# Subtracting the low halves of converted weights on VectorE instead of GpSimd, from the end of attention on

## The chip, the cores and the metric

The kernel runs on one core of a Trainium2 chip. The metric is the device time of one execution, in microseconds (us); lower is better. A core has four engines that compute, each with an instruction queue of its own that it works through in order: TensorE (matmul and transpose), VectorE, ScalarE and GpSimd. SyncE issues the transfers. In the profile they are called PE (PEld for its weight loads), DVE, ACT, POOL and SP.

## The reference

Attention with rotary embedding over 4 batches of 8 heads, 576 positions of 64 channels; its output, 2304 tokens of 512 channels, goes through two feed-forward blocks. The inputs come as float64 for the weights of the blocks, and the result is float32.

```python
scores = np.matmul(q_rot, k_rot.transpose(0, 1, 3, 2)) / np.sqrt(D)
attn = softmax(scores)                       # over the last axis
x = (attn @ v).transpose(0, 2, 1, 3).reshape(2304, 512)
h = x @ w_in                                 # 512 -> 2048
x2 = (h - np.tanh(h)) @ w_out                # 2048 -> 512
a, b = x2 @ w1, x2 @ w2                      # 512 -> 1024, twice
out = ((a * b) @ w3) @ w_o2                  # 1024 -> 1024 -> 512
```

## The kernel before, in words

TensorE works on a reduced float32 type. To keep accuracy each operand is kept as two halves: the high half is the value rounded to that type, the low half is what is left, value minus high half. A product of two operands is three matmuls: high by high, high by low, low by high.

*Weights.* They arrive as raw float64 words in units of 128 x 512. `load_raw` issues a unit's transfer into one of two `raw` buffers. `to_f32` makes float32 of it with two ScalarE instructions (L117, L119) and two VectorE instructions (L120, L122), in one of three `z` buffers. `split` makes the halves: the high one is a ScalarE copy (L127), the low one a subtraction (L128) on GpSimd. `next_conv` calls `to_f32` for the next unit of a fixed order and issues the next load; `place` and `conv_o2` call `split`. There are 16 units each in the first, second and third half of the weights (w_in and w_out twice, then w1 and w2), and 8 units of w_out2. The 16 units of w3 are not split here: they are transposed on TensorE and multiplied with w_out2 (`wp_trans`, `wp_mm`, L615 to L642), so that the second block needs one product less; L642 is a subtraction on GpSimd of its own.

*Attention.* 80 steps, one for each block of queries. A step has the scores (L325), their maximum on VectorE (L329), the exponential on ScalarE (L336), the scaling by the reciprocal of the sum on GpSimd (L347), transposes (L383, L393) and, for every second or third step, the product with v (L407, L410). Every sixth step converts and places one unit of the first half, nine units in all.

*The first block.* 80 chunks: two halves of the 2048 hidden channels, in each half five blocks of tokens (four of 512 and one of 256), in each block eight chunks of 128 hidden channels. `emit_h` is the product with w_in (L546, 12 matmuls), `emit_g` makes h - tanh(h) with four ScalarE instructions (L559 to L562), four VectorE instructions (L563 to L566), and splits the result with a ScalarE copy (L568) and a VectorE subtraction (L569). `emit_x2` is the product with w_out (L583, 12 matmuls). h and g are made two chunks ahead of x2. Behind each chunk stands what `at` put there: the seven units that are left of the first half in chunks 0 to 3, w_out2 in chunks 3 to 6 of the half, the folding of w3 after it, and the units of the next half from chunk 25 of the half on, at most two per chunk near its end. The tokens x are split too, by `split_x`, both instructions on GpSimd (L528, L529), into six buffers of which one block takes four.

*The second block.* 40 chunks: a and b (L750), their product on VectorE (L756), its split (L758 on ScalarE, L759 on VectorE), the last product (L773).

The order on each engine isn't wholly the order of the program text: the framework plans every queue at build time with costs of its own, and moves an instruction ahead when its inputs are there, of the units left from the first half, for example, some into attention. It also picks the engine of a copy that is written with `nc.any`.

Of the kernel before, what the change touches and what calls it, by code (L numbers as in the profile page):

```python
# [13 lines left out]
ALU = mybir.AluOpType  # L14
# [29 lines left out]
def fused_kernel(tc, q, k, v, w_in, w_out, w1, w2, w3, w_o2, tables, out):  # L44
    nc = tc.nc
# [13 lines left out]
    def f32(ap):  # L59
        return ap.bitcast(F32)  # L60
# [45 lines left out]
    def to_f32(u, z=None):  # L106
# [16 lines left out]
            z, hi, -0x80000000, z, ALU.bitwise_and, ALU.bitwise_or)  # L123
        return z.bitcast(F32)

    def split(z, s):
        nc.scalar.copy(s[:, 0, :], z)  # L127
        nc.gpsimd.tensor_tensor(s[:, 1, :], z, f32(s[:, 0, :]), ALU.subtract)  # L128


    pairs = [(b, hp) for b in range(B) for hp in range(NP)]
# [311 lines left out]
    def place(u):  # L443
        s = slot(slot_of[u], u)
        split(zs.pop(u), s)
        wslot[u] = s
# [63 lines left out]
            pv(b, hp, c // 2)  # L510
    att.release()
    psum.release()


    ph2 = tc.alloc_tile_pool(name="ph2", bufs=2, side="right", reuse_waits="tile")
# [83 lines left out]
    def conv_o2(i, r):  # L599

        u = next_conv()
        if r % 2 == 0:

            if i == 0:
                t = ph2.tile([128, 2, 2, 512], F32R, tag=f"x2{3 - r // 2}", name=f"o2_{i}{r}", bufs=1)
            else:
                t = xpool.tile([128, 2, 2, 512], F32R, tag=f"x{r // 2}", name=f"o2_{i}{r}")
            o2[i, r], o2[i, r + 1] = t[:, 0], t[:, 1]
        split(zs.pop(u), o2[i, r])
# [250 lines left out]
```

## Time and profile before

| | us |
|---|---|
| median of 3 runs | 1117.77 (1115.21 to 1119.29) |
| the profiled execution | 1111.25 |
| its span, from the first to the last instruction | 1109.4 |

| engine | busy in the span | instructions |
|---|---|---|
| TensorE | 95% | 5598 |
| TensorE weight loads | 77% | 5598 |
| VectorE | 66% | 1300 |
| ScalarE | 54% | 1262 |
| GpSimd | 35% | 379 |

Attention takes the first 323 us, the first block goes to about 809 us, the second to the end. A busy share says how much of a stretch an engine had an instruction running; an instruction that is held up while it runs counts as busy. In a view of instructions, idle time stands in brackets with what ended it.

### The profile page before, as it was taken

How to read it: one execution, taken by the hardware profiler on the slowest of the kernel's cores; microseconds unless marked ns; L12 is line 12 of the kernel's file. 1: busy time of each engine (PE TensorE's matmuls, PEld its weight loads, DVE VectorE, ACT ScalarE, POOL GpSimd, SP SyncE). 2: the span in 40 equal slices, each digit the busy share in tenths (PEclk: the TensorE clock that was granted, in tenths of full speed). 3: DMA queues.
4: the chain of work that ended last, by engine and by line, in shares of the span. 5: the costliest groups of instructions: out<-in, count | busy, mean ns of one | idle time of the engine just before them, and what ended most of it. 6: DMA issues, size and time to landing. Idle time of an engine off the chain costs nothing.

```text
span 1109.4 us, 15634 instructions
## 1 busy us (share of the span) xinstructions
PE 1055.3 (95%) x5598; PEld 853.6 (77%) x5598; DVE 730.3 (66%) x1300; ACT 598.9 (54%) x1262; POOL 387.8 (35%) x379
## 2 busy tenths in 40 slices
PE   5999999999998999998989999999799999999998
PEld 3777776777766888887767788898588888888887
DVE  6899988999649867669998867678952212212121
ACT  4688777777767655557767655556652111111121
POOL 5576675665461302014463220323630202001000
PEclk9899999999998999999999999999999999999999
DMA  6667675766403011023223102232740100101010
GB/s 195 171 161 173 182 178 140 186 176 147 99 20 106 10 57 58 32 64 95 77 76 113 38 10 76 87 105 86 246 133 1 38 1 1 38 1 38 1 38 20
DMA packets 64684, 96.36 MB, mean 87 GB/s; under 512 B 11616, under 2 KB 40288, under 8 KB 64608
## 3 DMA queue, kind: packets, MB, share of 16 engines
q1 hardware_dynamic: 64608, 95.38, 30.0%
q8 instruction: 44, 0.72, 0.3%
q14 instruction: 32, 0.26, 0.1%
HBM read 58.79 MB, written 11.01 MB: 63 GB/s over the span
## 4 chain that ended last, share of the span: by engine, by line
PE 68%; DVE 14%; ACT 7%; POOL 4%; DMA 4%; issue 2%; SPq 0%; DVEq 0%; ACTq 0%; POOLq 0%
PE pw L750 18%; PE x2p L583 11%; PE h L546 10%; PE o L773 9%; PE sc L325 6%; PE pv L410 4%; PE wp L630 3%; PE te L383 3%; DVE nm L329 2%; DMA raw_w<-in_moe_w 2%; DVE g_q L564 2%; ACT e L336 1%; DVE g_q L566 1%; PE pv L407 1%; DVE g_s L563 1%
## 5 line engine op out<-in xcount | busy, mean ns | idle before, releaser
L583 PE MATMUL x2p<-g,s_out 128*128 128x512 f32 (+1 forms) x960 | 223.4, 380 | 22.3 <-ACT g L568 12.8
L583 PEld LDWEIGHTS x2p<-g,s_out 128*128 128x128 f32 x960 | 172.2, 194 | 62.8 <-ACT g L568 18.3
L347 POOL TENSOR_SCALAR e<-e,r 128x576 f32<-128x576 f32 x144 | 121.8, 859 | 80.9 <-DVE r L345 35.8
L756 DVE TENSOR_TENSOR ab<-a,pw 128x512 f32<-128x512 f32 (+1 forms) x40 | 25.4, 635 | 182.9 <-PE pw L750 180.5
L336 ACT ACTIVATE e<-sc,nm 128x576 f32<-128x576 f32 x144 | 108.0, 750 | 47.2 <-DVE nm L329 31.5
L329 DVE TENSOR_REDUCE nm<-sc 128x1 f32<-128x576 f32 x144 | 106.8, 749 | 17.3 <-PE sc L325 16.5
L773 PE MATMUL o<-wpt,abs 128*128 128x512 f32 x432 | 104.5, 389 | 0.0
L325 PE MATMUL sc<-ks,qs 128*128 128x288 f32 x480 | 92.1, 321 | 3.2 <-ACT e L336 2.8
L563 DVE TENSOR_TENSOR g_s<-g_s,h 128x512 f32<-128x512 f32 (+1 forms) x80 | 50.5, 632 | 65.8 <-ACT g_m L562 65.6
L773 PEld LDWEIGHTS o<-wpt,abs 128*128 128x128 f32 x432 | 80.6, 188 | 16.4
L325 PEld LDWEIGHTS sc<-ks,qs 128*128 128x128 f32 x480 | 68.8, 190 | 26.7 <-ACT e L336 10.6
L383 PE MATMUL te<-ident,e 128*128 128x128 f32 x576 | 84.4, 278 | 5.1 <-POOL e L347 4.5
L754 ACT COPY a<-pw 128x512 f32<-128x512 f32 (+1 forms) x40 | 21.8, 544 | 117.9 <-PE pw L750 117.9
L568 ACT CAST g<-g_q 128x512 fp32r<-128x512 f32 (+1 forms) x80 | 46.1, 576 | 59.0 <-DVE g_q L566 58.6
L383 PEld LDWEIGHTS te<-ident,e 128*128 128x128 f32 x576 | 68.0, 142 | 11.7 <-POOL e L347 8.4
L559 ACT ACTIVATE g_s<-h 128x512 f32<-128x512 f32 (+1 forms) x80 | 44.1, 551 | 53.9 <-PE h L546 52.4
L569 DVE TENSOR_TENSOR g<-g_q,g 128x512 fp32r<-128x512 f32 (+1 forms) x80 | 58.1, 726 | 22.6 <-ACT g L568 21.7
L566 DVE COPY_PREDICATED g_q<-g_m,g_t 128x512 f32<-128x512 int32 (+1 forms) x80 | 69.1, 864 | 1.6
L758 ACT CAST abs<-ab 128x512 fp32r<-128x512 f32 (+1 forms) x40 | 23.0, 576 | 84.8 <-DVE ab L756 84.8
L564 DVE SCALAR_TENSOR_TENSOR g_q<-g_q,g_s 128x512 f32<-128x512 f32 (+1 forms) x80 | 62.6, 782 | 0.0
L560 ACT ACTIVATE g_q<-g_s,qb 128x512 f32<-128x512 f32 (+1 forms) x80 | 54.5, 682 | 0.2 <-DVE g L569 0.2
L562 ACT ACTIVATE g_m<-g_s,nt 128x512 f32<-128x512 f32 (+1 forms) x80 | 54.0, 676 | 0.0
(380 smaller groups left out, 2256.7 us busy)
## 6 DMA issues: line engine op xcount, KB each, us to landing
ks<-kp SPq DMA_DIRECT2D x60, 288.0 KB, 5.0
raw_w<-in_moe_w SPq DMA_DIRECT2D x32, 512.0 KB, 3.7
raw_in<-in_moe_w_in SPq DMA_DIRECT2D x16, 512.0 KB, 4.0
raw_out<-in_moe_w_out SPq DMA_DIRECT2D x16, 512.0 KB, 4.4
qs<-qp SPq DMA_DIRECT2D x60, 128.0 KB, 3.5
wp_dram<-wpe SPq DMA_DIRECT2D x24, 256.0 KB, 2.0
k<-in_k SPq DMA_DIRECT2D x16, 256.0 KB, 3.2
q<-in_q SPq DMA_DIRECT2D x16, 256.0 KB, 3.0
```

The lines of the kernel that those rows point to most:

```text
L325: nc.tensor.matmul(s[:, n, 0:HS], lhs, rhs, start=t == 0, stop=t == len(terms) - 1)
L329: nc.vector.tensor_reduce(nm[:, j:j + 1], s[:, :, 0:HS], AX.XY, ALU.max, negate=True)
L336: nc.scalar.activation(d["e"][:, j, :].rearrange("p (n s) -> p n s", n=2), d["ss"][j][:, :, 0:HS], AF.Exp, bias=d["nm"][:, j:j + 1], accum ...
L347: nc.gpsimd.tensor_scalar(d["e"][:, j, :], d["e"][:, j, :], r[:, j:j + 1], 1.0, ALU.mult, ALU.mult)
L383: nc.tensor.transpose(ps[:, n * 128:(n + 1) * 128], e[:, o + n * 128:o + (n + 1) * 128], ident)
L546: nc.tensor.matmul(ps[:, 0:w], ws[:, a, kk], x[:, b_, 0:w], start=kc == 0 and t == 0, stop=kc == NK - 1 and t == 2)
L563: nc.vector.tensor_tensor(s, s, h, ALU.mult)
L564: nc.vector.scalar_tensor_tensor(qq, qq, QC, s, ALU.add, ALU.mult)
L566: nc.vector.copy_predicated(qq, mk.bitcast(I32), t)
L583: nc.tensor.matmul(x2ps[j][o][:, 0:w], ws[:, a, oo], g[:, b_, 0:w], start=c == 0 and t == 0, stop=c == HF - 1 and t == 2)
L750: nc.tensor.matmul(ps[:, 0:w], ws[:, a, kk], x[:, b_, 0:w], start=kc == 0 and t == 0, stop=kc == NK - 1 and t == 2)
L773: nc.tensor.matmul(outps[j][t], g[:, a, tt], wp[c][:, b_, :], start=c == 0 and i == 0, stop=c == NF2 - 1 and i == 2)
```

## The change

A list of one element holds the engine that subtracts the low half. It is GpSimd until all of attention has been written, and VectorE from there on. All calls of `split` after the attention loop therefore emit their subtraction for VectorE. `split_x` (L528, L529) and L642 stay on GpSimd, L127 stays on ScalarE.

```diff
+    lows = [nc.gpsimd]
+
     def split(z, s):
         nc.scalar.copy(s[:, 0, :], z)
-        nc.gpsimd.tensor_tensor(s[:, 1, :], z, f32(s[:, 0, :]), ALU.subtract)
+        lows[0].tensor_tensor(s[:, 1, :], z, f32(s[:, 0, :]), ALU.subtract)
...
     att.release()
     psum.release()
+    lows[0] = nc.vector
```

## Rows read from the trace of the kernel before

**Rows 1.** The page, its first part: busy time of each engine.
```profile
PE 1055.3 (95%) x5598; PEld 853.6 (77%) x5598; DVE 730.3 (66%) x1300; ACT 598.9 (54%) x1262; POOL 387.8 (35%) x379
```

**Rows 2.** Stretches: length, busy (instructions) PE PEld DVE ACT POOL, clock, DMA.
```profile
0.00:323.00 323.00, 298.51 (x2028) 224.61 (x2030) 277.03 (x637) 233.32 (x590) 197.99 (x216) 0.98 0.61 157
323.00:345.00 22.00, 17.82 (x70) 13.88 (x67) 17.83 (x18) 13.95 (x25) 13.11 (x11) 0.84 0.14 48
345.00:505.00 160.00, 159.91 (x788) 134.88 (x787) 114.10 (x182) 95.77 (x179) 26.67 (x25) 1.00 0.17 54
515.00:585.00 70.00, 62.76 (x263) 48.44 (x262) 64.38 (x84) 51.84 (x93) 34.10 (x25) 0.98 0.26 79
585.00:630.00 45.00, 42.04 (x179) 32.79 (x178) 38.38 (x55) 31.71 (x57) 15.38 (x13) 1.00 0.25 81
752.00:806.00 54.00, 47.08 (x208) 38.44 (x207) 48.40 (x63) 36.93 (x66) 24.41 (x19) 0.95 0.50 171
806.00:845.00 39.00, 39.00 (x170) 32.16 (x170) 20.65 (x29) 18.16 (x32) 11.37 (x9) 0.98 0.29 94
```

**Rows 3.** The same view of the GpSimd instructions of L128 alone.
```profile
0.00:323.00 323.00, 19.05 (x14) 0.98 0.61 157
515.00:585.00 70.00, 23.05 (x16) 0.98 0.26 79
752.00:806.00 54.00, 11.51 (x8) 0.95 0.50 171
```

**Rows 4.** Line L128: durations min/median/max in ns; who waited for it.
```profile
L128 POOL TENSOR_TENSOR s_in<-z_in,s_in x14: 1272/1302/1751, 24.7 to 573.7; 128x512 fp32r<-128x512 f32 x14
  ACT z_in L117: 8.5, 3
```

**Rows 5.** Timeline from 323 to 345: start, length, instruction, [idle before, releaser].
```profile
323.58 0.62 ACT L127 CAST s_out<-z_out 128x512 fp32r<-128x512 f32 x1 [2.53 <-issue]
326.64 1.31 POOL L128 TENSOR_TENSOR s_in<-z_in,s_in 128x512 fp32r<-128x512 f32 x1
327.42 4.75 DVE L120 SCALAR_TENSOR_TENSOR z_o<-z_o,raw_o 128x512 int32<-128x512 int32 x1 [3.42 <-ACT z_o L117]
329.22 0.72 ACT L562 ACTIVATE g_m<-g_s,nt 128x512 f32<-128x512 f32 x1
331.00 0.64 POOL L528 TENSOR_SCALAR xs_(0, 1)_1_4659<-x 128x512 fp32r<-128x512 f32 x1
333.80 0.67 DVE L563 TENSOR_TENSOR g_s<-g_s,h 128x512 f32<-128x512 f32 x1
337.89 2.07 PE L583 MATMUL x2p<-g,s_out 128*128 128x512 f32 x4 [4.18 <-ACT g L568]
```

**Rows 6.** Timeline of one chunk, 540 to 548, VectorE and GpSimd.
```profile
541.38 1.19 DVE L564 SCALAR_TENSOR_TENSOR g_q<-g_q,g_s 128x512 f32<-128x512 f32 x1
541.99 1.74 POOL L128 TENSOR_TENSOR s_in<-z_in,s_in 128x512 fp32r<-128x512 f32 x1
542.77 1.51 DVE L120 SCALAR_TENSOR_TENSOR z_out<-z_out,raw_out 128x512 int32<-128x512 int32 x1 [0.19 <-ACT z_out L117]
545.44 0.68 DVE L120 SCALAR_TENSOR_TENSOR z_in<-z_in,raw_in 128x512 int32<-128x512 int32 x1
546.04 0.68 DVE L569 TENSOR_TENSOR g<-g_q,g 128x512 fp32r<-128x512 f32 x1
```

**Rows 7.** Timeline from 553 to 569, GpSimd, TensorE and ScalarE.
```profile
554.88 1.30 POOL L128 TENSOR_TENSOR s_out<-z_out,s_out 128x512 fp32r<-128x512 f32 x1 [2.52 <-ACT s_out L127]
561.66 1.04 PE L546 MATMUL h<-xs_(1, 0)_3_6402,s_in 128*128 128x512 f32 x2 [2.20 <-POOL xs_(1, 0)_3_6402 L529]
567.87 0.67 ACT L117 ACTIVATE z_in<-raw_in 128x512 f32<-128x512 f32 x1 [4.86 <-POOL s_out L128]
```

**Rows 8.** Stretches as in rows 2, at lowered clock.
```profile
336.70:343.40 6.70, 5.51 (x13) 4.34 (x14) 6.60 (x10) 5.27 (x10) 1.60 (x1) 0.50 0.22 83
562.00:565.20 3.20, 3.20 (x9) 2.46 (x8) 3.20 (x6) 1.01 (x2) 3.12 (x3) 0.50 0.46 147
```

## The prediction

> **What bounds the kernel now.** I first read the busy shares [rows 1]: TensorE is busy for 95% of the span, VectorE for 66%, GpSimd for 35%. An average of this kind hides stages, so next come the stretches [rows 2]. From 345 to 505 us TensorE is busy for 159.91 of 160.00 us: there it is the bound, and work taken from or given to VectorE changes nothing, but a delay or a gain made before 345 is carried through. The change can matter only where TensorE waits: 323 to 345 (busy 17.82 of 22.00), 515 to 585 (62.76 of 70.00), 585 to 630 (42.04 of 45.00) and 752 to 806 (47.08 of 54.00). In 515 to 585 and 752 to 806 VectorE has little room left: 64.38 of 70.00 and 48.40 of 54.00. So the change adds work to VectorE exactly where VectorE is fullest, and the question is how much of that fullness is work, and how much is VectorE held up by GpSimd.
>
> The timeline of one chunk answers this [rows 6]. L569, a VectorE subtraction of the same shape and types as the one that moves, took 0.68 us undisturbed, and L120 also took 0.68. Beside a GpSimd L128, L120 took 1.51 and L564 took 1.19; these read two tensors from SBUF. The GpSimd side pays as well: 1.74 us against a median of about 1.30 [rows 4]. The worst case is at 327.42, where one L120 took 4.75 us while five GpSimd instructions went by, two of them L128 and three of them splits of x (the first and the last stand in [rows 5]).
>
> **The change part by part.** *Count.* Of the 56 low halves, 9 are placed inside the attention loop and stay on GpSimd. The other 47 move: 7 left over from the first half, 8 of w_out2, 16 and 16 of the second and third half. Before 323 us there are 14 instances of L128 [rows 3], so 5 of the moved ones were put into attention by the planner; 42 lie after it.
>
> *Removed from GpSimd:* 47 x 1.30 = 61 us of an engine with much idle time, worth nothing in itself. *Added to VectorE:* 47 x about 0.60 us. The instruction lasts 0.68, but in a full queue the next starts 0.60 later (545.44 to 546.04 [rows 6]). That is 28 us: 3 in attention, 3.6 around 323 to 350, 9.6 in 515 to 585 (16 instances [rows 3]), 2.4 in 585 to 630, 4.8 in 752 to 806 (8 instances), 4.8 after.
>
> *Removed from VectorE:* the stretching by L128. In the chunk of rows 6 two units are placed, and the two stretched instructions lost 1.51 - 0.68 = 0.83 and 1.19 - 0.68 = 0.51, together 1.34 us, 0.67 per unit. I take 0.6 per moved unit in the full stretches; the bounds are 0 (a unit placed in idle time) and 1.3 (a whole GpSimd instruction). So 0.60 comes and about 0.6 goes. VectorE's time in 515 to 585 and 752 to 806 stays about equal; collisions of the new subtractions with the GpSimd splits of x, which stay, add some 1 to 2 us in all. The load alone is worth between -2 and +4 us; I take +1.
>
> *Stalls that go.* (a) At 323 to 345. The copies before three moved subtractions begin at 323.58, when VectorE has nothing queued that is long; there they can be done some 2 us before GpSimd did them. L120 at 327.42 then meets the splits of x alone. L563 need not wait till 333.80: its last input, L562, is there at 329.22 + 0.72 = 329.94. That is 3.86 us earlier, against 4.18 us of TensorE waiting at 337.89 [rows 5]. I take 3.5, bounds 0 (the splits of x alone keep VectorE out as long) and 4.2. In 336.70 to 343.40 the granted clock was 0.50, that is 1.2 instead of 2.4 GHz [rows 8]; it fell after this wait of TensorE, and it cost half of 6.7 us, 3.4. With a wait under 1 us it may not fall: I take 2, bounds 0 and 3.4. (b) At 561.66 TensorE waited 2.20 us for a split of x on GpSimd. That split came late because L128 stood ahead of it in GpSimd's queue: GpSimd idled 2.52 us for its ScalarE copy and then spent 1.30 on it [rows 7]. With L128 gone the split is done 3.8 us earlier, so the 2.20 goes, and perhaps the 1.6 us which half a clock from 562.00 to 565.20 cost [rows 8]. ScalarE's wait of 4.86 us for a z buffer held by a backed-up L128 [rows 7], of 8.5 us in three such waits [rows 4], goes too, but VectorE is then the next one late: I count 3 for all of (b), bounds 0 and 5. (c) 585 to 630 and 752 to 806: the stalls there come with splits of x and with VectorE's own queue; I count 0, bounds -2 and +3. (d) Attention: 5 x 0.60 more on VectorE, busy 277.03 of 323.00, against 5 x 1.30 less on GpSimd: 0, bounds -1.5 and +2. (e) 806 to 845: VectorE is busy 20.65 of 39.00 and TensorE all 39.00 [rows 2]; 0, bounds 0 and +3.
>
> *One rule against a row.* At 327.42 VectorE was kept out through several GpSimd instructions in a row, 4.75 - 0.68 = 4.07 us [rows 5]. The Trainium skill (SBUF — State Buffer, "SBUF: two separate sides") calls the pair of ports that both engines share an exclusive lock, held for the whole instruction by whichever starts first, which alone would end a wait after the one instruction that is running. By that rule a moved subtraction loses at most one GpSimd instruction, and the load term would end at +2 instead of +4. The row is the longer one and I keep its value for the upper end: a moved subtraction that meets a chain of splits can be held for up to 4 us.
>
> **Sum.** +1 (load) - 3.5 - 2 (a) - 3 (b) + 0 (c, d, e) = -7.5; I take -7, since two terms lean on the next engine being on time. The profiled execution took 1111.25 us, so it would take 1104. The runs shown have a median of 1117.77, 6.5 above that execution; the difference is put onto the median: 1117.77 - 7 = 1111.
>
> **The rivals.** *R1: VectorE takes back what the stalls give.* Waits vanish, but VectorE, with 5.62 us idle in 515 to 585, is the bound there all the same, and the gain at 323 shrinks to 2 or 3 us because the splits of x hold VectorE as before. For it: of the five instructions that L120 waited for at 327.42, three are splits of x [rows 5]. Against it: the balance of 0.60 against 0.67 per unit. Time: -3 to +4, about 1117.
>
> *R2, slower: a new wait at the head of VectorE's queue.* The moved subtraction needs the ScalarE copy L127, which needs L122 on VectorE. GpSimd could sit waiting for L127 at no cost; VectorE cannot, since its queue is in order and L563 to L569 of the next chunk stand behind it. Place: chunks with two units, 515 to 585 and 752 to 806. If nothing useful is queued between L122 and the subtraction, each costs 0.60 plus the copy's 0.62 [rows 5], about 1.2: 24 x 1.2 = 29, minus 24 x 0.6 removed, is 14 more; the idle time of VectorE there (5.6 + 5.6 [rows 2]) covers part of it, as long as it isn't the same idle time that TensorE waits for. With (a) still gained: +7 us, 1125. It decides from about 0.4 us of waiting per moved unit. For it: ScalarE too has a queue, with weight loads ahead. Against it: the planner fills such places, and in the chunk of rows 6 other VectorE work stands there.
>
> *R3: all stalls go, the clock stays up, and VectorE has time left:* -12 to -16, about 1104.
>
> That the change does not do what it says has no room here: the switch is set before the first of the 47 is placed; only where the planner puts them is open.
>
> **How the numbers follow.** Chances: forecast (-4 to -11, around 1111) 0.50; R1 0.25; R2 0.18; R3 0.07. About 0.5%, 5.6 us, is what a measurement of this kernel can tell from no change. Of the forecast's half, 0.38 lies beyond 5.6 us and 0.12 within. Faster: 0.38 + 0.07 = 0.45. Same: 0.12 + 0.25 = 0.37. Slower: 0.18. The range goes from 1102 (R3's far end) to 1125 (the middle of R2); half of R2 (0.09) and some 0.03 below 1102 stay outside, so it should hold a little more than 8 in 10; the terms with bounds on both sides (a, b, the load) make it no narrower.
>
> **What would show it.** Right: no L128 on GpSimd after attention except the nine; L120, L122, L564 and L566 near 0.7 us except beside splits of x; the wait of TensorE near 334 us under 1 us and no half clock after it; no wait of TensorE for a split of x near 560. R1: those stalls shrink, but TensorE's busy share in 515 to 585 stays near 62.76 of 70.00. R2: VectorE idle just ahead of the moved subtractions, ended by L127, over 0.4 us each, and ScalarE waiting for L566 longer than before. The prediction would be wrong by its own steps if the planner orders attention or the chunks otherwise because VectorE now carries the cost, so that places in the timeline no longer answer to each other.

## The result and the profile after

| | before | after |
|---|---|---|
| median, us | 1117.08 (1115.21 to 1119.29) | 1103.62 (1098.54 to 1106.90) |
| the profiled execution, us | 1111.25 | 1106.90 |
| its span, us | 1109.4 | 1105.0 |

The ratio after to before is 0.9875, with an interval from 0.9832 to 0.9918; measured a second time beside the experiments it is 0.9911 (0.9877 to 0.9944). The change makes the kernel about 1% faster, 13.5 us by the medians above. The two profiled executions differ by 4.4 us only; why they show so little of it is said below.

In the changed kernel all line numbers from L127 on are larger: the copy is L129, the low half L130, the split of x L531 and L532, the product with w_in L549, `emit_g` L562 to L572, the product with w_out L586.

The page after, its first part (answers to [rows 1]):
```profile
PE 1060.1 (96%) x5598; PEld 857.8 (78%) x5598; DVE 734.1 (66%) x1344; ACT 599.8 (54%) x1265; POOL 324.2 (29%) x332
```
GpSimd lost 63.6 us and 47 instructions, as counted. VectorE has 44 more (47 subtractions, less three copies that went to ScalarE, 1262 to 1265) and is busy only 3.8 us longer.

The stretches after, with the columns and the times of [rows 2] (length, busy with count of PE, PEld, DVE, ACT, POOL, granted clock, DMA share, GB/s):
```profile
323.00:345.00 22.00, 17.14 (x83) 12.95 (x82) 15.68 (x20) 13.88 (x27) 11.59 (x11) 0.96 0.15 48
345.00:505.00 160.00, 159.89 (x769) 133.76 (x769) 112.73 (x178) 93.37 (x174) 25.12 (x24) 0.99 0.15 50
515.00:585.00 70.00, 67.90 (x304) 55.57 (x303) 66.18 (x102) 53.55 (x97) 14.39 (x12) 0.98 0.22 68
585.00:630.00 45.00, 41.87 (x171) 33.67 (x171) 43.16 (x64) 31.18 (x56) 9.65 (x8) 0.92 0.26 82
752.00:806.00 54.00, 48.59 (x206) 38.46 (x205) 50.71 (x75) 35.30 (x62) 11.01 (x9) 0.94 0.51 174
```
TensorE is busy 67.90 of 70.00 us in 515 to 585, and was 62.76. Its busy time in the other stretches differs by less than 2 us from that before. The work inside a stretch is not quite the same, since the whole run is shifted; so I also take the two parts of the kernel by their own ends.

The first block, from the first matmul of the product with w_in to the end of the last with w_out, before:
```profile
323.44:809.07 485.63, 461.12 (x2179) 381.04 (x2178) 380.76 (x557) 304.31 (x563) 154.04 (x128) 0.98 0.23 77
```
and after:
```profile
327.19:804.58 477.39, 459.24 (x2179) 382.02 (x2178) 381.53 (x590) 303.35 (x562) 105.00 (x94) 0.98 0.24 79
```
It is 8.24 us shorter. TensorE's idle time in it (length less busy) fell from 24.51 to 18.15 us. VectorE ran 33 instructions more in 0.77 us more of busy time: what it lost in held-up time paid for them.

Attention, from the 61st score matmul to the last product with v, before:
```profile
45.68:323.51 277.83, 265.33 (x1878) 201.72 (x1876) 243.77 (x560) 210.12 (x535) 175.34 (x184) 0.99 0.60 152
```
and after:
```profile
54.03:327.26 273.23, 263.64 (x1878) 200.83 (x1876) 242.57 (x563) 210.97 (x537) 171.94 (x179) 1.00 0.62 155
```
That is 4.60 us shorter. The second block is the same to 0.02 us. So this pair differs by 8.24 + 4.60 = 12.8 us, which fits the ratio; 1.3 us of the 4.60 are not the change's, as (d) below shows. The start of the profiled execution after, ahead of these 61 matmuls, took 8.35 us longer than before (54.03 against 45.68), with the same instructions in the same order; that hides most of the gain in the spans. It is the subject of the last section.

TensorE's waits after, by what ended them, 323 to 806 (us in total, times, longest; one of 0.5 us that belongs to attention is left out):
```profile
PE x2p L586 <- ACT g L571: 9.1, 4, 4.4
PE x2p L586 <- DVE g L572: 8.4, 7, 2.4
PE x2p L586 <- DVE x L596: 0.3, 1, 0.3
```
The wait for a split of x of 2.20 us [rows 7] is gone. The longest one is still there, and it is the one that the prediction meant to remove.

Timeline after, 326 to 343 (start, length, instruction, idle before and its releaser), answers to [rows 5]:
```profile
327.99 1.72 DVE L130 TENSOR_TENSOR s_out<-z_out,s_out 128x512 fp32r<-128x512 f32 x1 [0.23 <-ACT s_out L129]
331.17 1.72 POOL L532 TENSOR_TENSOR xs_(0, 1)_0_4596<-x,xs_(0, 1)_0_4596 128x512 fp32r<-128x512 f32 x1
331.66 3.47 DVE L120 SCALAR_TENSOR_TENSOR z_o<-z_o,raw_o 128x512 int32<-128x512 int32 x2
335.77 0.62 ACT L129 CAST o<-z_o 128x512 fp32r<-128x512 f32 x1 [4.33 <-DVE z_o L122]
338.63 0.69 DVE L566 TENSOR_TENSOR g_s<-g_s,h 128x512 f32<-128x512 f32 x1 [1.51 <-ACT g_m L565]
342.30 0.98 PE L586 MATMUL x2p<-g,s_out 128*128 128x512 f32 x3 [4.38 <-ACT g L571]
```
The moved subtractions now collide with the splits of x (1.72 us instead of 0.68), two L120 behind them take 3.47 us beside L532, ScalarE stands 4.33 us on a weight copy that needs their result, and the four ScalarE instructions of the first chunk stand behind that copy. TensorE waits 4.38 us, before 4.18.

Line L130 after 323 us, what the engine waited for ahead of it (us, times):
```profile
  ACT s_w L129: 0.7, 1
  ACT s_out L129: 0.2, 1
```
42 subtractions and 0.9 us of waiting for their copies: 0.02 us each.

### The profile page after: what moved, and what is told of

Same layout as the page of the kernel before. It is cut to its first block, busy times and chain, and to the rows that moved or that the text cites. A ratio compares the mean times of both kernels' runs of the same rounds, so it can differ in the third digit from the quotient of the medians.

```text
span 1105.0 us, 15609 instructions
## 1 busy us (share of the span) xinstructions
PE 1060.1 (96%) x5598; PEld 857.8 (78%) x5598; DVE 734.1 (66%) x1344; ACT 599.8 (54%) x1265; POOL 324.2 (29%) x332
## 4 chain that ended last, share of the span: by engine, by line
PE 69%; DVE 15%; ACT 7%; DMA 4%; issue 3%; POOL 1%; DVEq 0%; ACTq 0%; SPq 0%; POOLq 0%
PE pw L753 18%; PE x2p L586 11%; PE h L549 10%; PE o L776 9%; PE sc L327 7%; PE pv L412 4%; PE wp L633 3%; PE te L385 3%; DVE nm L331 2%; ACT e L338 2%; DMA raw_in<-in_moe_w_in 2%; DVE g_q L569 1%; DVE g_q L567 1%; DVE g L572 1%; PE pv L409 1%
## 5 line engine op out<-in xcount | busy, mean ns | idle before, releaser
L586 PE MATMUL x2p<-g,s_out 128*128 128x512 f32 (+1 forms) x960 | 221.5, 379 | 18.1 <-ACT g L571 9.1
L586 PEld LDWEIGHTS x2p<-g,s_out 128*128 128x128 f32 x960 | 171.9, 193 | 55.9 <-DVE g L572 13.6
L349 POOL TENSOR_SCALAR e<-e,r 128x576 f32<-128x576 f32 x144 | 125.1, 881 | 86.6 <-DVE r L347 46.4
L566 DVE TENSOR_TENSOR g_s<-g_s,h 128x512 f32<-128x512 f32 (+1 forms) x80 | 50.5, 631 | 61.6 <-ACT g_m L565 61.5
L562 ACT ACTIVATE g_s<-h 128x512 f32<-128x512 f32 (+1 forms) x80 | 44.1, 551 | 53.8 <-PE h L549 53.7
L572 DVE TENSOR_TENSOR g<-g_q,g 128x512 fp32r<-128x512 f32 (+1 forms) x80 | 57.4, 717 | 23.3 <-ACT g L571 22.8
L569 DVE COPY_PREDICATED g_q<-g_m,g_t 128x512 f32<-128x512 int32 (+1 forms) x80 | 61.1, 764 | 1.0
L567 DVE SCALAR_TENSOR_TENSOR g_q<-g_q,g_s 128x512 f32<-128x512 f32 (+1 forms) x80 | 55.0, 687 | 0.0
L563 ACT ACTIVATE g_q<-g_s,qb 128x512 f32<-128x512 f32 (+1 forms) x80 | 54.6, 682 | 0.4 <-DVE g L572 0.4
```

The costliest lines, as they stand in the source:

```text
L349: nc.gpsimd.tensor_scalar(d["e"][:, j, :], d["e"][:, j, :], r[:, j:j + 1], 1.0, ALU.mult, ALU.mult)
L567: nc.vector.scalar_tensor_tensor(qq, qq, QC, s, ALU.add, ALU.mult)
L569: nc.vector.copy_predicated(qq, mk.bitcast(I32), t)
L572: nc.vector.tensor_tensor(g[:, 1, 0:w], qq, f32(g[:, 0, 0:w]), ALU.subtract)
L586: nc.tensor.matmul(x2ps[j][o][:, 0:w], ws[:, a, oo], g[:, b_, 0:w], start=c == 0 and t == 0, stop=c == HF - 1 and t == 2)
```

## The experiments

Two theories stood at first. Theory A: the gain is made unit by unit, where a low half on GpSimd held a VectorE operation or stood ahead of a split of x. Theory B: it comes from another plan of the queues. Below, a VectorE operation is called stretched by what it lasted beyond the lower quartile of its line and shape; the sum is over the first block, and what is under 0.05 us is left out. A stretch is put down to the GpSimd instructions that ran beside it, by the length of the overlap. The table holds what was read from the runs: ratio to the kernel before, and from each trace the length of attention and of the first block (with the same ends as above), TensorE's idle time in the block, the time there at a granted clock of 0.50, and the stretch.

| kernel | ratio (95%) | attention | first block | TensorE idle | clock 0.50 | VectorE stretch |
|---|---|---|---|---|---|---|
| before | 1 | 277.83 | 485.63 | 24.51 | 17.1 | 50.9 |
| the change | 0.9875 (0.9832, 0.9918) | 273.23 | 477.39 | 18.15 | 20.5 | 33.6 |
| the change again | 0.9911 (0.9877, 0.9944) | 273.12 | 477.67 | 19.50 | 17.1 | 32.2 |
| first third only | 0.9994 (0.9966, 1.0023) | 273.06 | 486.67 | 25.51 | 17.1 | 46.2 |
| middle third only | 0.9938 (0.9912, 0.9965) | 276.40 | 476.25 | 18.29 | 17.1 | 38.6 |
| last third only | 1.0006 (0.9976, 1.0035) | 277.18 | 483.07 | 20.61 | 17.1 | 44.4 |
| no low halves | 0.9788 (0.9741, 0.9834) | 273.24 | 467.04 | 12.59 | 6.8 | 28.7 |
| w_out2 due later | 0.9907 (0.9877, 0.9937) | 273.13 | 476.54 | 18.18 | 17.1 | 34.2 |
| low half of x alone | 0.9941 (0.9911, 0.9970) | 276.37 | 476.97 | 17.47 | 10.2 | 33.0 |
| change and low half of x | 0.9684 (0.9643, 0.9726) | 273.13 | 452.89 | 3.97 | 0 | 9.2 |
| change and all of x | 0.9718 (0.9680, 0.9756) | 273.21 | 454.84 | 4.93 | 0 | 1.9 |
| change, low x, all low halves | 0.9721 (0.9677, 0.9764) | 273.84 | 453.80 | 4.65 | 0 | 8.6 |
| change and two-input scratch | 1.0149 (1.0109, 1.0189) | 271.80 | 504.69 | 33.56 | 34.1 | 60.6 |
| change and one-input scratch | 0.9996 (0.9966, 1.0025) | 272.52 | 489.01 | 23.76 | 23.9 | 43.3 |

### Which of the moved units bring the gain

Three kernels move one part each; the first:
```diff
-    def split(z, s):
+    def split(z, s, u):
         nc.scalar.copy(s[:, 0, :], z)
-        lows[0].tensor_tensor(s[:, 1, :], z, f32(s[:, 0, :]), ALU.subtract)
+        low = lows[0] if u in half1 + fold[0] else nc.gpsimd
+        low.tensor_tensor(s[:, 1, :], z, f32(s[:, 0, :]), ALU.subtract)
```


> Only the 7 units left over from the first half and the first 4 of w_out2 subtract their low halves on VectorE (11 of the 47); the other 36 stay on GpSimd. Theory A (the gain lies in 515 to 600 us, where VectorE is no longer held up by L128 and the splits of x no longer queue behind it on GpSimd): this part shows only the re-planned attention, -1 to -5 us, 1112 to 1116; the TensorE wait of about 4.3 us behind the first chunk stays. Theory B (the gain is the re-planned attention): nearly the whole gain, 1102 to 1106.

This one moves the seven units that are left of the first half and four of w_out2. The second has `u in half2 + fold[1]` (16 units of the second half, converted from about 508 us on, and four of w_out2), the third `u in half3` (16 units).

> Only the 16 units of the second half and the last 4 of w_out2 subtract on VectorE (20 of 47). Theory A: -6 to -10 us, 1107 to 1111, with TensorE busy over 66 of 70 us in 515 to 585. Theory B: 1116 to 1118, since attention keeps its GpSimd subtractions.

> Only the 16 units of the third half subtract on VectorE. Theory A: 0 to -3 us, 1114 to 1117, since the waits of TensorE near 793 us come with the splits of x, which stay. Theory B: 1116 to 1118. Rival R2 of the prediction (a new wait in VectorE's queue) would show here first: slower by 2 to 4 us.

The middle third measures 0.9938 and the others cannot be told from no change. Its trace has the whole gain of the first block (476.25 against 485.63), with TensorE in 515 to 585 as in the changed kernel:
```profile
515.00:585.00 70.00, 67.20 (x304) 55.39 (x305) 66.43 (x105) 54.72 (x99) 10.87 (x9) 1.00 0.24 76
```
The first third has, by its trace, all of the gain in attention (273.06) and nothing in the block; its ratio alone can't tell this from no change. So there are two separate gains, at two places: theory A holds for the larger, in the block, and attention has one of its own. The last third shows no loss of 2 to 4 us, as R2 would have it. By the measured ratios the parts add up to 0.9938; the whole measured 0.9875 once and 0.9911 once, so whether it is more than its parts stays open.

### How much the low halves cost at all

```diff
-    lows[0] = nc.vector
+    lows[0] = lambda *a: None
...
-                nc.tensor.matmul(ps[:, 0:w], ws[:, a, kk], x[:, b_, 0:w],
+                nc.tensor.matmul(ps[:, 0:w], ws[:, 0, kk], x[:, b_, 0:w],
```
(The other products with split weights are changed alike: the matmul count stays, the low halves of the 47 units are neither made nor read.)

> The 47 low halves are not computed at all, and every product that would read the low half of a weight reads the high half in its place, so that TensorE does as many matmuls of the same shape; this leaves a part of the computation out. It is the bound of what a free subtraction would give. If VectorE pays for the 47 subtractions (my sum: 28 us of its time, of which little shows), this is 3 to 8 us under the changed kernel, 1096 to 1100; if they cost nothing there, it is equal to it, about 1104; if the gain had been used up by them (R1), it is far below, 1090 or less.

It measures 0.9788. So the 47 subtractions cost the kernel before 2.1% where they were, some 23.6 us, and about half of that still where they are now (0.9788 against 0.9875 and 0.9911: 0.9 to 1.2%, 10 to 14 us, 0.2 to 0.3 us a unit). That is more than the 3 to 8 us that were expected; the first blocks of the two traces, 467.04 and 477.39 us, differ by 10.35.

### The changed kernel again

> The changed kernel once more, beside the next three on the same chip, so that its ratio has as many rounds as those of the parts. The low halves of the first third alone gave 0.9994, of the middle third 0.9938, of the last third 1.0006. Theory A (the gain is made where a low half on GpSimd holds a VectorE operation and the splits of x, unit by unit): the parts add up, ratio 0.993 (0.990 to 0.996). Rival B (the parts help one another, since GpSimd comes free for the splits of x only when all are gone, and the plan of attention is another one): ratio 0.9875 as first measured, 6 us better than the sum of the parts.

0.9911, inside theory A's range (0.990 to 0.996); rival B's 0.9875 lies just below the interval, which begins at 0.9877. By itself this does not rule B out. Its trace tells more than its ratio: attention and first block come out as in the first trace to 0.3 us, and its start took 45.50 us up to the 61st score matmul, as in the kernel before, so that its span is 1096.6 us.

### The wait behind the first chunk

```diff
-FOLD_AT, FOLD_EVERY = (3, 10), 2.25
+FOLD_AT, FOLD_EVERY = (5, 10), 2.25
```


> The changed kernel with the conversions of w_out2 due from the fifth place on and not the third. It asks why TensorE's wait of 4.4 us behind the first chunk (337.91 to 342.30) stayed. Theory D (it stays because the planner sets two units of w_out2 ahead of the first chunk's eviction on VectorE, with the splits of x against the moved subtractions): the wait falls under 2 us, 2 to 4 us faster than the changed kernel, ratio 0.984 to 0.986. Rival: the wait is the splits of x behind the moved subtractions, and stays over 3.5 us; ratio as the changed kernel's, within 0.3%.

The wait stays at 4.39 us and the ratio at 0.9907, the figures of the rival. But this decides nothing: the later due place did not move the two L120, which stand in the same order ahead of the first chunk's L566 and last 3.47 us again. The next kernel settles it.

### The splits of x

```diff
         nc.gpsimd.tensor_scalar(t[:, 0, 0:w], src[:, kc, :], 1.0, 1.0, ALU.mult, ALU.mult)
-        nc.gpsimd.tensor_tensor(t[:, 1, 0:w], src[:, kc, :], f32(t[:, 0, 0:w]), ALU.subtract)
+        nc.vector.tensor_tensor(t[:, 1, 0:w], src[:, kc, :], f32(t[:, 0, 0:w]), ALU.subtract)
```


> The changed kernel with the low half of x too on VectorE; the high half stays on GpSimd. Of the 14.5 us that TensorE still waits behind attention in the changed kernel, all stand beside splits of x on GpSimd. Theory A (what is left of the loss is VectorE kept out by these splits, some 33 us of stretched VectorE operations, as it was by the low halves of the weights): 3 to 8 us faster than the changed kernel, ratio to the kernel before 0.981 to 0.985. Rival C (VectorE is full: its busy time in the stretch 515 to 585 is 66 of 70 us by now, so 40 more subtractions of about 0.6 us cost more than the port gives back): 0 to 8 us slower than the changed kernel, ratio 0.988 to 0.995.

0.9684: three times the gain of the change, and far past the expectation of theory A, which counted on a part of TensorE's waits alone and left the half clock out. Rival C falls. The first block of this kernel:
```profile
323.00:775.89 452.89, 448.92 (x2179) 376.51 (x2178) 376.30 (x628) 305.02 (x564) 42.47 (x48) 1.00 0.25 82
```
VectorE has 71 instructions more than in the kernel before (628 against 557) and is busy 4.46 us less. TensorE's idle time falls from 18.15 to 3.97 us, and its busy time by 10.32 us with the same 2179 matmuls; no part of the block is at half clock any more (20.5 us were, which cost half of that, 10.2). In the timeline of its first chunk nothing is held up:
```profile
325.89 0.68 DVE L130 TENSOR_TENSOR s_out<-z_out,s_out 128x512 fp32r<-128x512 f32 x1
329.51 0.69 DVE L566 TENSOR_TENSOR g_s<-g_s,h 128x512 f32<-128x512 f32 x1
333.74 1.43 PE L586 MATMUL x2p<-g,s_out 128*128 128x512 f32 x5
```
L566 begins 6.5 us after the block's start, with the change alone 11.4, and TensorE does not wait. So the wait behind the first chunk was that of VectorE beside the splits of x.

With the high half on ScalarE as well, GpSimd has nothing of x left:
```diff
-        nc.gpsimd.tensor_scalar(t[:, 0, 0:w], src[:, kc, :], 1.0, 1.0, ALU.mult, ALU.mult)
+        nc.scalar.copy(t[:, 0, 0:w], src[:, kc, :])
```


> The changed kernel with the whole split of x off GpSimd: the high half is a ScalarE copy, the low half a VectorE subtraction. Theory A: no VectorE operation is stretched behind attention any more, the waits of TensorE at the heads of the chunks go, 5 to 12 us faster than the changed kernel, ratio 0.977 to 0.983. Rival C: the high halves queue behind the weight copies on ScalarE (some 40 copies of 0.6 us, 23 us) and the low halves behind the products' evictions on VectorE; the chunks begin later, 0 to 10 us slower than the changed kernel, ratio 0.988 to 0.996.

0.9718, faster than theory A's range (0.977 to 0.983); rival C falls. But it is not better than the step before it. The stretch goes from 9.2 to 1.9 us and TensorE's idle time does not fall (4.93), so taking the one-input halves off GpSimd brings nothing more that can be seen, at 18.6 us more on ScalarE (323.61 against 305.02 in the first block). How one VectorE line fares is seen in its row of the page (busy, mean ns, idle before); the copy with a mask, before:
```profile
L566 DVE COPY_PREDICATED g_q<-g_m,g_t 128x512 f32<-128x512 int32 (+1 forms) x80 | 69.1, 864 | 1.6
```
with the change:
```profile
L569 DVE COPY_PREDICATED g_q<-g_m,g_t 128x512 f32<-128x512 int32 (+1 forms) x80 | 61.1, 764 | 1.0
```
and with the change and the low half of x:
```profile
L569 DVE COPY_PREDICATED g_q<-g_m,g_t 128x512 f32<-128x512 int32 (+1 forms) x80 | 56.3, 704 | 0.8
```

Next the same line in the kernel before, the weights' low halves left on GpSimd:
```diff
-        nc.gpsimd.tensor_tensor(t[:, 1, 0:w], src[:, kc, :], f32(t[:, 0, 0:w]), ALU.subtract)
+        nc.vector.tensor_tensor(t[:, 1, 0:w], src[:, kc, :], f32(t[:, 0, 0:w]), ALU.subtract)
```


> The kernel before with one line changed: the low half of x on VectorE, the low halves of the weights left on GpSimd. The change alone measured 0.9875 and 0.9911, both moves together 0.9684. In the trace of the kernel before, VectorE operations behind attention are stretched by 50.9 us, of which 19.5 stand beside low halves of weights and 30.3 beside splits of x. Theory A (each two-input subtraction on GpSimd costs by the VectorE time that it stretches, and the two kinds add): 2.0 to 2.5% without the change, ratio 0.975 to 0.980, and the change on top of it brings about 1%. Rival E (the loss is made where both kinds meet on GpSimd's queue, so taking away either one is nearly enough): ratio 0.968 to 0.972, as with both. Rival F (the low halves of weights on GpSimd then hold more VectorE work than before, since VectorE is fuller): ratio over 0.982.

0.9941. Theory A in its simple form, that the two costs add, is wrong: the change alone brings 0.9 to 1.25%, the low half of x alone 0.6%, both 3.2%. Rival E is wrong too, and F's bound holds, though not for its reason: the stretch by low halves of weights stays at 19.3 us (19.5 before). In the first block the two single moves bring 8.2 and 8.7 us, both 32.7. At the first chunk it can be seen why one move is not half of two. Timeline of this kernel there:
```profile
331.47 1.77 DVE L529 TENSOR_TENSOR xs_(0, 0)_1_4319<-x,xs_(0, 0)_1_4319 128x512 fp32r<-128x512 f32 x1
332.65 1.74 POOL L128 TENSOR_TENSOR s_in<-z_in,s_in 128x512 fp32r<-128x512 f32 x1
335.87 1.77 DVE L120 SCALAR_TENSOR_TENSOR z_o<-z_o,raw_o 128x512 int32<-128x512 int32 x1
```
Whichever of the two kinds stays on GpSimd stretches what the other put onto VectorE. TensorE waits 4.18 us there before, 4.38 with the change, 0.73 + 0.72 + 2.53 with the low half of x alone, nothing with both. The half clock in the block goes from 17.1 us to 20.5 and 10.2 with one of them, and to zero with both. Beyond the first chunk this reading is argued from the sums of the table, not shown wait by wait.

### GpSimd's work put back, with no product waiting for it

```diff
+        if ghost[0] is not None:
+            for k in (slice(0, 256), slice(256, 512)):
+                nc.gpsimd.tensor_tensor(ghost[0], z[:, k], f32(s[:, 0, k]), ALU.subtract)
```


> The changed kernel, in which GpSimd also subtracts each of the moved low halves in two pieces of 128x256 into a scratch buffer that nobody reads: GpSimd has its two-input work of before back, and no one waits for the result. Theory A (the loss of before is VectorE kept out, and splits of x queued, while GpSimd runs a two-input subtraction; not the wait for its result): nearly the whole gain behind attention goes, and VectorE has the added subtractions besides: ratio 0.997 to 1.006. Rival G (the loss of before was the late low half itself, for which a product waited): the gain stays, ratio 0.988 to 0.992.

1.0149, past even the loss that theory A gave. Rival G, that a product waited for the late low half, falls: no product reads these results. Something does wait, though: a `z` buffer comes free only when the scratch work has read it, and ScalarE stood for that in the block (us in total, times, longest):
```profile
ACT z_in L117 <- POOL ghost L134: 7.8, 2, 4.4
ACT z_out L117 <- POOL ghost L134: 3.8, 1, 3.8
```
Together these are 11.6 us; the kernel before has 14.2 of the same kind behind L128, the one-input kernel below 4.7. How much of the loss comes by this way and how much by VectorE's stretch was not separated. The block:
```profile
321.95:826.64 504.69, 471.13 (x2179) 384.40 (x2178) 413.18 (x599) 313.10 (x578) 185.42 (x172) 0.97 0.24 80
```
VectorE is busy 31.65 us longer than with the change, with nine instructions more. A part of the surplus is that pieces of 256 take 0.73 us at least, 1.46 a unit, against 1.30 for one of 512 [rows 4].

The same with one input, four pieces for a unit:
```diff
+                for _ in range(2):
+                    nc.gpsimd.tensor_scalar(ghost[0], z[:, k], 1.0, 1.0, ALU.mult, ALU.mult)
```


> As the kernel with two-input scratch work, but GpSimd runs in their place four one-input multiplications by 1 of 128x256 for each moved low half, about as long on GpSimd (four times some 0.31 us against two times 0.65). It keeps GpSimd's queue as full without a second input. Theory A1 (what costs is the two-input form, which keeps VectorE out; the queue is a smaller part): ratio 0.990 to 0.994. Rival H (what costs is that the splits of x stand behind other work in GpSimd's queue, whatever its form): as with the two-input scratch work, within 0.3%.

0.9996: between A1 and H, and neither. GpSimd is busy even longer than with two inputs (block, POOL column, 200.70 against 185.42):
```profile
322.46:811.47 489.01, 465.25 (x2179) 382.54 (x2178) 395.81 (x599) 311.90 (x577) 200.70 (x250) 0.98 0.25 82
```
yet it costs 1.0% and not 2.6% over the change (taken at the mean of its two ratios). So the two-input form costs more by the microsecond, as A1 has it (part of the difference may be the waits for `z` buffers, 11.6 against 4.7 us): 25.9 us of VectorE's stretch stand beside the 78 two-input pieces, 0.33 each, and 14.6 beside 156 one-input pieces, 0.09 each (counts: GpSimd's in the block less the 94 of the changed kernel). But occupation of GpSimd is not free either, and two waits of TensorE for a split of x are back in both kernels (2.3 and 2.2 us with two inputs, 0.8 and 2.2 with one).

### The rest of attention

```diff
-    lows = [nc.gpsimd]
+    lows = [nc.vector]
```
(with the low half of x on VectorE)

> The changed kernel with the low half of x on VectorE, as measured at 0.9684, and in addition the nine low halves of weights that GpSimd still takes in the first part of attention moved to VectorE. Theory A (a low half on GpSimd costs wherever it stands; five of them moved in attention shortened attention by some 4.6 us): 3 to 8 us faster, ratio 0.961 to 0.966. Rival C (from 60 to 174 us VectorE is busy for 108 of 114 us, and TensorE waits for it at each row maximum): 0 to 5 us slower, ratio 0.968 to 0.973.

0.9721 against 0.9684 without it, the intervals overlap widely: no gain shown, and the value lies in rival C's range. Attention takes 273.84 us against 273.13. The nine further low halves bring nothing there (VectorE is busy for 108.34 of 114.00 us from 60 to 174 in the changed kernel), so a low half on GpSimd does not cost "wherever it stands".

The best kernel is the change with the low half of x on VectorE, 1078.06 us beside 1113.83 for the kernel before.

## Why the prediction was right, and where its steps were not

Faster was the likeliest of the three, and 1103.62 lies in the range, 7.4 below the predicted 1111, close to R3's 1104. By the steps:

- **The load, +1 (-2 to +4): right.** VectorE's busy time in the first block rose by 0.77 us for 33 more instructions. No moved subtraction was held for 4 us: the longest after lasted 1.78, so 1.10 over its 0.68, less than one GpSimd subtraction. For the upper bound the rule of the Trainium skill (SBUF — State Buffer, "SBUF: two separate sides"), that a loser waits for the one instruction that holds the lock, was the better guide: this trace agrees, with 1.10 us beside it. The long row of before does not, and it is not alone. The kernel with two-input scratch work has one more, beside six GpSimd instructions in a row:
```profile
326.62 5.00 DVE L120 SCALAR_TENSOR_TENSOR z_in<-z_in,raw_in 128x512 int32<-128x512 int32 x1 [7.29 <-ACT z_in L117]
```
  What decides between one instruction and a chain is open.
- **(a), -3.5 and -2: failed.** The step was "L120 at 327.42 then meets the splits of x alone", from which L563 was let start at 329.94. With L128 gone the splits of x were enough to hold the moved subtractions and two L120, and a ScalarE copy that waited for L120's successor stood ahead of L562. The wait went from 4.18 to 4.38. The lower bound, 0, had named this case. Half clock behind it fell from 6.83 to 3.41 us, which is worth 1.7, about the 2 that was taken.
- **(b), -3 (0 to -5): right in kind, too small.** From the 29th to the 45th chunk of the product with w_out (502.99 to 600.55 before, 507.11 to 595.78 after) the kernel gained 97.56 - 88.67 = 8.9 us. The split of x came in time, as put. The stretch before:
```profile
502.99:600.55 97.56, 87.36 (x387) 68.30 (x385) 89.62 (x121) 71.46 (x133) 46.93 (x34) 0.98 0.28 88
```
  and after:
```profile
507.11:595.78 88.67, 84.10 (x385) 69.25 (x385) 84.14 (x131) 68.14 (x127) 19.79 (x16) 0.98 0.25 79
```
  What was missing are the other waits of this stretch: the prediction counted one TensorE wait and its half clock, and set the stretching by L128 against the added subtractions as if VectorE's sum were all that counts. L128 had stretched VectorE by 10.0 us in 515 to 600. The chunks' own VectorE operations (L563 to L566 and L569, 81 before and 82 after), which the products with w_out wait for, took 65.5 us before and 56.7 after; the sixteen moved subtractions took 11.4. In VectorE's sum these nearly cancel, as was put (the rows are lower after by the conversions of some three units too, which fall outside). For TensorE they do not: its idle time fell from 10.20 to 4.57 us. That the one brings the other is argued here, not shown wait by wait.
- **(c), 0: right in sum.** Chunks 45 to 51 lost 2.0 us, at splits of x near 607; the last chunks, from the 71st on, gained 1.8.
- **(d) attention, 0 (-1.5 to +2): wrong**, 4.60 us faster. Of these 1.3 are not the change's. The trace of the kernel before has a stretch at half clock in attention that no other trace has:
```profile
148.90:152.30 3.40, 3.40 (x14) 2.81 (x12) 2.09 (x7) 2.21 (x6) 3.18 (x4) 0.50 0.38 118
```
  The time from its 261st to its 281st score matmul is 13.91 us, against 12.60 to 12.63 in all others but the last experiment's (12.19). That holds for the middle third, the last third and the low half of x alone too, which moved no weight unit in attention and run the same instructions there in the same order (the low half of x alone up to the splits of x at its end). The other 3 to 4 us come with the five moved units: attention lasts 276.37 to 277.18 us in those three kernels and 273.06 to 273.24 in the seven that have the five units off GpSimd and neither scratch work nor a further move of weights. The step that failed is that 5 x 1.30 us less on GpSimd was put at nothing. The scaling of the exponentials stands in GpSimd's queue there, and TensorE's transposes wait for it; their row of the page before:
```profile
L383 PE MATMUL te<-ident,e 128*128 128x128 f32 x576 | 84.4, 278 | 5.1 <-POOL e L347 4.5
```
and after:
```profile
L385 PE MATMUL te<-ident,e 128*128 128x128 f32 x576 | 84.6, 279 | 3.7 <-POOL e L349 2.8
```
  That is 1.7 us of it. Why nine more units bring nothing is open.
- **(e), 0: right**, the second block, to the last instruction, is 300.4 us in both.
- **R1** was right on its place, the first chunk, and wrong on the sum. **R2** needed 0.4 us of waiting per moved unit; there were 0.02. **R3** has the size, but not its reason: stalls and half clock stayed (18.15 us idle, 20.5 us at half clock); both go only with the splits of x.

The forecast's sum was 7.5; measured in the traces are 12.8: -0.6 up to the 5th chunk, (a); +0.9 up to the 29th, at splits of x near 510; -8.9 (b); +0.3 (c); -4.6 (d), 1.3 of it the half clock of one execution, which leaves 11.5 for the change. Two misses of opposite sign, (a) and (b), nearly cancelled, which is luck, and (d) is most of the difference.

## What to carry to other kernels

When GpSimd and VectorE work on the same stage, read VectorE's busy time as work plus hold-ups: compare each line's mean with its shortest instances, and ask which GpSimd instruction stands beside the long ones. A subtraction that takes 0.68 us on VectorE can be cheaper there than on an idle GpSimd, even where VectorE is the fuller engine. If two kinds of GpSimd work stretch the same queue, try both moves together before judging either: one alone brought 1%, the other 0.6%, both 3.2%.

## What was not expected of the hardware

The start of the kernel is not the same from one execution to the next. TensorE, 20 to 42 us, in the kernel before (columns as in the stretches above):
```profile
20.00:30.00 10.00, 9.50 (x45) 6.11 (x45) 9.13 (x22) 7.01 (x19) 5.60 (x7) 0.97 0.74 175
30.00:42.00 12.00, 12.00 (x58) 8.48 (x57) 8.81 (x22) 5.50 (x15) 6.14 (x7) 0.74 0.49 141
```
and in the changed kernel:
```profile
20.00:30.00 10.00, 10.00 (x28) 5.82 (x27) 5.56 (x14) 4.89 (x15) 3.74 (x4) 1.00 0.41 100
30.00:42.00 12.00, 12.00 (x35) 7.94 (x35) 7.15 (x16) 6.15 (x15) 4.30 (x5) 1.00 0.63 157
```
TensorE is busy nearly all the time in both and does 103 matmuls in one and 63 in the other. In the timeline eight score matmuls of one shape take 2.35 us in the kernel before:
```profile
22.09 2.35 PE L325 MATMUL sc<-k_first,q_first 64*128 64x288 f32 x8
```
and four of them 2.29 in the changed one:
```profile
22.82 2.29 PE L327 MATMUL sc<-k_first,q_first 64*128 64x288 f32 x4
```
Twice the time for each. The column of the granted clock, 1.00 at both places, misleads here. The trace of the changed kernel has no record of the clock before 42.9 us, that of the kernel before none before 15.8, and the view counts a stretch without a record as 1.00. What the clock was can be read from eight transposes of one shape. In the kernel before, first at a recorded 1.00, then in its stretch at 0.50 (29.4 to 36.2 us):
```profile
24.37 1.09 PE L383 MATMUL te<-ident,e 128*128 128x128 f32 x8
33.69 1.91 PE L383 MATMUL te<-ident,e 128*128 128x128 f32 x8
```
In the changed one, first ahead of any record, then across the beginning of the first:
```profile
30.03 1.97 PE L385 MATMUL te<-ident,e 128*128 128x128 f32 x8
42.59 1.18 PE L385 MATMUL te<-ident,e 128*128 128x128 f32 x8
```
Those ahead of the record take the time of those at 0.50. So TensorE, though busy, ran at the lower of its two levels up to 42.9 us in this execution, and up to 15.8 in the other. The other traces agree. Of the fourteen, thirteen have the same instructions in the same order up to the 61st score matmul. It starts at 45.50 and 45.68 us in the two whose records begin at 15.6 and 15.8, at 49.60 to 50.22 in five (30.4 to 31.1), and at 53.07 to 54.23 in six (41.7 to 43.1). In the two of the changed kernel it starts at 45.50 and 54.03, so this is not the change's; what sets the time of the first full clock was not tried.

It means that two spans of single executions can't be subtracted here. The stages behind the start repeat better: attention and first block do to 0.3 us in the two traces of the changed kernel. The kernel before was traced once, and there is the half clock in attention; its shortest span, 1103.4 us, is 6.0 below that of its trace, which has one of the earliest starts. So its stages vary too, and differences of a few us against that one trace are less sure than the ratios.
